# A RetNet recurrence feeding a SiLU feed-forward layer: how the remainders of split operands are formed, four buffers for g, and the reload of chunk 2's x

## The chip, the cores and the metric

The kernel runs on one core of one Trainium2 chip. The metric is the device time in microseconds of one execution; lower is better. TensorE (PE) multiplies, and loads its weights on a second track (PEld). VectorE (DVE), ScalarE (ACT) and GpSimd (POOL) work element by element, and SyncE (SP) issues all DMAs, in one queue.

## The reference

```
# q, k, v: (4, 8, 768, 64); gamma[h] = 1 - 2**(-5-h); scale = 1/8
for t in range(768):
    state = gamma * state + outer(k[:, :, t], v[:, :, t])
    y[:, :, t] = scale * q[:, :, t] @ state
x = y.transpose(0, 2, 1, 3).reshape(3072, 512)
h = x @ w_in            # 512 x 2048
g = h * sigmoid(h)
out = g @ w_out         # 2048 x 512
```

The inputs are given to the kernel as 64-bit words; it builds 32-bit floats from them where they are weights.

## The kernel before, in words

The sequence is cut into six chunks `c` of 128 steps, and four batches `b` give 24 units `n = 4c + b`. A unit's attention has three stages, visited one behind another: `visit(m)` runs the transposes of unit m (`stage_t`, for early units on PE), the scores and state sums of unit m-1 (`stage_s`, `stage_a`), and the outputs of unit m-2 (`stage_y`). From unit 14 (`FAR`) on the transposes are made by DMA instead: `part_t` (POOL copies), `turn_t` (two DMA transposes, to tiles kw and qw), `join_t` (ACT copies).

A chunk's four y make x^T of that chunk. Every operand of the two large products is kept in three parts (high, low, and a scaled combination), so that three products of rounded numbers give the accuracy of one of full ones. So a product (c, f), with f one of the 16 slices of w_in, has 12 matmuls of 512 columns: 8 into bank `ha`, 4 into `hb` (`multiply`, L749). `close_steps` (L775) takes them out: ACT copies `ha` to an SBUF tile `g` (L777), DVE subtracts `hb` (L782), and `put_g` stores `g` to DRAM. `turn` hands out three PSUM banks in rotation, `h0` to `h2`; four others hold attention's tiles, tagged s and y, and one, q, is used by the early transposes and at the very end.

The order of the products is written out in `steps`: chunks 0 and 1 with the early slices, chunk 2 with slices 0 to 7 among them, then `last`: (0, 12) to (0, 15), (1, 12) to (1, 15), (2, 8) to (2, 15), then chunks 3, 4 and 5. `behind[c, f]` gives the work that is issued behind a product; `visit(14)` stands behind (1, 15). PE's order is the program's; the orders of the other engines come from a scheduler, within the queues that `queue(...)` and `tc.issue_after` set. `behind_next` holds work for DVE behind the next drain.

`takes` names the products behind which one slice of weights is converted from 64-bit words (`convert_steps`, L199 to L231: two ACT and four DVE operations, the last a custom one on 16-bit words at L230). Slices of w_in are then split into parts (`split_steps`, L115): ACT makes the high part (L121), DVE a remainder into a tile `wl` (L124), ACT the low part by scaling the remainder (L127), DVE the third (L129). Slices of w_out go to DRAM and are read back and split the same way during chunk 5. The factor 1/8 of the reference is put into w_in's parts.

Chunk 2's x has no room to stay: its place is needed for the last four slices of w_in. Its four quarters go to DRAM (`y_dram`), and come back when chunk 0's x is done: `late_y(b)` reloads quarter b into a tile `yr`, `late_x(b)` splits it again (ACT high part L653, DVE L656 and L659). (2, 8) is the first product that reads the reloaded x, and every one of its matmuls reads columns of all four quarters. The tiles `kt` (two buffers) and `qt` (three) are shared among transposed k and q, the copies for the DMA transposes, and these reloads. A buffer is free when the last reader of its tile has run.

When all `g` are stored they are read back, put through SiLU and split (L843 to L847), and multiplied with w_out (L1270).

Of the kernel before, what the change touches and what calls it, by code (L numbers as in the profile page):

```python
# [12 lines left out]

FP32 = mybir.dt.float32
FP32R = mybir.dt.float32r
# [3 lines left out]
AF = mybir.ActivationFunctionType  # L19
ALU = mybir.AluOpType  # L20
# [8 lines left out]
EPS = 2.0 ** -12  # L29
# [5 lines left out]
def kernel(  # L35
# [46 lines left out]
    def pool(name, bufs, **kw):  # L82
        return ctx.enter_context(tc.tile_pool(name=name, bufs=bufs, **kw))
# [4 lines left out]
    const = pool("const", 1)  # L88
    ld = pool("ld", 2)
    one = pool("one", 1)  # L90
    hpool = pool("hpool", 3)
    stage = pool("stage", 2)
    conv = pool("conv", 1)
    ps_u = pool("ps_u", 1, space=PS)
# [17 lines left out]
            quads[name] = wpool.tile([128, 4, 3, 512], FP32R, tag="wq", name=f"{name}4")  # L112
        return quads[name][:, f - NF + 4]

    def split_steps(f, w32, name, factor, to, behind_x=False):  # L115

        to[f] = w = w_slot(f, name)
        lo = conv.tile([128, 512], FP32, tag="wl", name=f"{name}l_{f}")
        yield
        with queue((held or evac or [None])[0] if behind_x or f >= NF - 4 else evac[0]):  # L120
            nc.scalar.activation(out=w[:, 0, :], in_=w32, func=AF.Copy, scale=HALF * factor)  # L121
        high = w[:, 0, :].bitcast(FP32)
        yield
        nc.vector.scalar_tensor_tensor(out=lo, in0=w32, scalar=factor, in1=high,  # L124
                                       op0=ALU.mult, op1=ALU.subtract)
        yield
        nc.scalar.activation(out=w[:, 1, :], in_=lo, func=AF.Copy, scale=1.0 / EPS)  # L127
        yield
        nc.vector.scalar_tensor_tensor(out=w[:, 2, :], in0=high, scalar=EPS, in1=lo,  # L129
                                       op0=ALU.mult, op1=ALU.subtract)  # L130

    def split_w(*of):
        steps = split_steps(*of)
        next(steps)
        yield
        list(steps)
# [17 lines left out]
    def load(name, n):  # L154
        if n >= len(units):
            return
        c, b = units[n]
        src = {"k": k, "q": q, "v": v}[name]
        if n == 4 * B and name == "k":
            t = conv.tile([128, H, D], FP32, tag="wl", name=f"kf_{n}")  # L160
            nc.sync.dma_start(out=t, in_=src[b, :, ds(c * C, C)].rearrange("h t d -> t h d"))
            kqv[name][n] = t
            return
        if n < EARLY:

            if n not in early:
                early[n] = wpool.tile([128, 3, H, D], FP32, tag=f"w{4 + n}", name=f"kqv_{n}")
            t = early[n][:, "kqv".index(name)]
        else:
            t = ld.tile([128, H, D], FP32, tag=f"{name}f", name=f"{name}f_{n}",  # L170
                        bufs=2 if name == "q" else 3)
        nc.sync.dma_start(out=t, in_=src[b, :, ds(c * C, C)].rearrange("h t d -> t h d"))
        kqv[name][n] = t
# [76 lines left out]
    def early_slice(i):  # L250

        out = []
        yield from convert_steps(i, out)
        yield
        steps = split_steps(i, out[0], "wi", scale, w_sb, None)
        next(steps)
        yield from steps

# [9 lines left out]
    def take_w(after=None, parts=False):  # L268

        i = taken[0]  # L270
        taken[0] += 1
        if i >= 2 * NF:
            return
        with queue(after) if after else ExitStack():
            rounded = convert_w(i)

        def finish():
            w32 = rounded()
            if i < NF:
                list(split_w(i, w32, "wi", scale, w_sb))  # L280
            else:
                to_store.append((i - NF, w32))

        if parts:
            behind_next.append(finish)
        else:
            with queue(after) if after else ExitStack():
                finish()
# [13 lines left out]
    def begin_w():  # L302

        i = taken[0]
        taken[0] += 1
        split = split_w(i, convert_w(i)(), "wi", scale, w_sb, True)
        next(split)
        half_split.append(split)

# [93 lines left out]
    def turn(name):  # L403
        turns[0] += 1
        return ps_h.tile([128, 512], FP32, tag=f"h{turns[0] % 3}", name=name)
# [271 lines left out]
    y_late = {}  # L677

    def late_y(b):
        p, tag, bufs = ((one, "kt", 2), (conv, "wl", 1))[b % 2]  # L680
        y_late[b] = p.tile([128, KIN, C], FP32, tag=tag, name=f"yr_{b}", bufs=bufs)
        nc.sync.dma_start(out=y_late[b], in_=y_dram[b])

# [62 lines left out]
    def product_in(c, f):  # L746
        close_in(c, f, *multiply(c, f))

    def multiply(c, f):  # L749
        ha, hb = turn(f"ha_{c}_{f}"), turn(f"hb_{c}_{f}")  # L750
        fill(ha, FILL_P.get((c, f), 0))
        for i in range(3):
            for kk in range(KIN):
                nc.tensor.matmul(hb if i == 2 else ha, lhsT=w_sb[f][:, i, ts(kk, 128)],  # L754
                                 rhs=woven(xt[c][:, i, kk, :]), start=kk == 0 and i != 1,
                                 stop=kk == KIN - 1 and i != 0)
        return ha, hb
# [16 lines left out]

    def close_steps(c, f, ha, hb):  # L775
        hs = new_g(c, f)
        copied[:] = [nc.scalar.activation(out=hs, in_=ha, func=AF.Copy, scale=ONE_E).ins]  # L777
        with queue(copied[0]):
            while behind_copy:
                behind_copy.pop(0)()  # L780
        yield
        taken_out[:] = [nc.vector.tensor_tensor(out=hs, in0=hs, in1=hb, op=ALU.subtract).ins]  # L782
        with queue(taken_out[0]):
            while behind_next:
                behind_next.pop(0)()
        yield
        (later if (c, f) in kept_g else pending).append((c, f, hs))
# [31 lines left out]
            w_got[f] = t  # L819

    def w_out(f, parts=False):
        steps = split_steps(f, w_got.pop(f), "wo", 1.0, wo)
        for _ in range(3):
            next(steps)
        get_w(f + W_READ)
        if parts:
            behind_next.append(lambda: list(steps))
        else:
            list(steps)
# [323 lines left out]
    takes = [(1, 5)] + [(0, f) for f in range(6, half)]  # L1153
    takes += [(2, half - 4), (2, half - 2)]
    takes += [(0, half), (0, half + 3), (1, half + 1), (1, half + 3)]
    takes += [(0, NF - 3), (0, NF - 1), (1, NF - 3)]
    takes += [(3, f) for f in (0, 3, 7, 11, 14)]
    takes += [(4, f) for f in (0, 3, 7, 11, 14)]
    takes += [(5, f) for f in (2, 5, 8)]
# [6 lines left out]
    for i, x in enumerate(at):  # L1166
        behind[x] = lambda m=EARLY + 6 + i: visit(m)
    behind[0, NF - 2] = lambda: [late_y(b) for b in range(2)]
    behind[1, NF - 4] = lambda: [late_x(0), late_y(2), late_x(1), late_y(3)]
    behind[1, NF - 2] = lambda: [late_x(2), late_x(3)]  # L1170
    behind[1, NF - 1] = lambda: visit(EARLY + 6)


# [11 lines left out]
    put_later = {6: 1, 7: 2, 9: 1, 10: 1, 11: 1, 13: 1, 14: 1, 15: 1}  # L1185
    assert sum(put_later.values()) == len(kept_g)
    loads_at = {first_far + 4: [("k", FAR + 1), ("q", FAR + 1)], far[FAR] + 1: [("q", FAR + 2)]}
    for n, (c, f) in enumerate(steps):
        if n in scales_at:
            behind_next.append(lambda m=scales_at[n]: scale_k(m))  # L1190
        if n in joins_at:
            behind_copy.insert(0, lambda m=joins_at[n]: [join_t(name, m) for name in "qk"])
        if n in parts:
            behind_next.append(lambda m=parts[n]: part_t(m, taken_out[0]))
        patient[0] = steps.index((3, 0)) <= n < max(turns_at) + 2
        product_in(c, f)
        put_g(1)
        if n in put_later:
            put_g(len(later) - put_later[n], later)
        store_w()  # L1200
        if (c, f) in takes:
            take_w(taken_out[0], n < len(pairs + three) or c == NC - 1)
        behind.get((c, f), lambda: None)()
        if n in turns_at:
            turn_t(turns_at[n])
            if turns_at[n] >= LATER:
                with tc.issue_after(turned_by[0]):
                    load("k", turns_at[n] + 1), load("q", turns_at[n] + 1)
        if turns_at.get(n - 1, 0) >= LATER:
            with tc.issue_after(stored[0]):  # L1210
                load("v", turns_at[n - 1] + 1)
        if turns_at.get(n - 2, 0) >= LATER:
            with tc.issue_after(stored[0]):
                while waiting:
                    load_w(waiting.pop(0))
        for name, m in loads_at.get(n, ()):
            load(name, m)
        if c == NC - 1:
            if f == 0:
                for i in range(W_READ):  # L1220
                    get_w(i)
            if f < NF - 4:
                w_out(f, True)
            if f >= NF - 6:
                if f == NF - 6:
                    for n in range(G_AHEAD):
                        get(n)
                if f >= NF - S_AHEAD:
                    with tc.issue_after(taken_out[0]):
                        split(f - NF + S_AHEAD)  # L1230
# [124 lines left out]
```

## Time and profile before

| | |
|---|---|
| runs | 593.3, 593.84 and 3425.35 us; median 593.84 |
| the profiled execution | 592.68 us, its span 590.9 |
| PE, DVE, ACT, POOL busy | 579.3, 401.1, 342.7, 34.1 us |
| DMA | 108.91 MB, mean 184 GB/s |

The profile is of one execution. Times within it are microseconds from the start of the span. An engine's idle time matters only where another waits for it; PE's matters always where PE sets the end.

### The profile page before, as it was taken

How to read it: one execution, taken by the hardware profiler on the slowest of the kernel's cores; microseconds unless marked ns; L12 is line 12 of the kernel's file. 1: busy time of each engine (PE TensorE's matmuls, PEld its weight loads, DVE VectorE, ACT ScalarE, POOL GpSimd, SP SyncE). 2: the span in 40 equal slices, each digit the busy share in tenths (PEclk: the TensorE clock that was granted, in tenths of full speed). 3: DMA queues.
4: the chain of work that ended last, by engine and by line, in shares of the span. 5: the costliest groups of instructions: out<-in, count | busy, mean ns of one | idle time of the engine just before them, and what ended most of it. 6: DMA issues, size and time to landing. Idle time of an engine off the chain costs nothing. (4 is left out here: it accounts for less than half of the span.)

```text
span 590.9 us, 13700 instructions
## 1 busy us (share of the span) xinstructions
PE 579.3 (98%) x5509; PEld 498.2 (84%) x5509; DVE 401.1 (68%) x672; ACT 342.7 (58%) x607; POOL 34.1 (6%) x89
## 2 busy tenths in 40 slices
PE   8999999999999999999999999999999999999996
PEld 6787888888788888888888888888888888888885
DVE  3887999678896767767779794745645463645632
ACT  7787767576656446655477695544644544545311
POOL 3000120100022111120000000000000000000000
PEclk9999999999999999999999999999999999999999
DMA  9989877786699699999667863532524433443301
GB/s 193 214 198 207 191 194 266 251 251 215 202 263 222 174 269 245 285 258 253 236 207 276 265 214 107 175 111 91 194 73 138 147 108 106 158 127 102 113 1 72
DMA packets 144336, 108.91 MB, mean 184 GB/s; under 512 B 101136, under 2 KB 109584, under 8 KB 144272
## 3 DMA queue, kind: packets, MB, share of 16 engines
q1 hardware_dynamic: 144272, 108.03, 65.3%
q8 instruction: 43, 0.70, 0.5%
q14 instruction: 21, 0.17, 0.1%
HBM read 66.06 MB, written 36.70 MB: 174 GB/s over the span
## 5 line engine op out<-in xcount | busy, mean ns | idle before, releaser
L754 PE MATMUL ha<-xt,wi 128*128 128x512 f32 x736 | 176.6, 382 | 0.6 <-DVE g L782 0.4
L754 PEld LDWEIGHTS ha<-xt,wi 128*128 128x128 f32 x736 | 137.1, 189 | 22.6 <-DVE g L782 2.6
L1270 PE MATMUL o<-wo,gs 128*128 128x512 f32 x564 | 137.1, 379 | 0.0
L1270 PEld LDWEIGHTS o<-wo,gs 128*128 128x128 f32 x564 | 106.6, 189 | 15.1
L846 DVE TENSOR_TENSOR gs<-gr,gs 128x512 fp32r<-128x512 f32 x96 | 62.1, 685 | 83.1 <-ACT gs L844 83.1
L1270 PE MATMUL oa<-wo,gs 128*128 128x512 f32 x376 | 111.8, 379 | 0.0
L843 ACT ACTIVATE gr<-gr 128x512 f32<-128x512 f32 x96 | 59.6, 629 | 65.5 <-DMA gr<-gd 64.2
L754 PE MATMUL hb<-xt,wi 128*128 128x512 f32 x368 | 95.0, 380 | 1.8 <-DVE gk L782 0.9
L777 ACT ACTIVATE g<-ha 128x512 f32<-128x512 f32 x87 | 51.8, 596 | 64.1 <-PE ha L754 49.8
L782 DVE TENSOR_TENSOR g<-g,hb 128x512 f32<-128x512 f32 x87 | 59.5, 684 | 41.7 <-ACT g L777 34.6
L754 PEld LDWEIGHTS hb<-xt,wi 128*128 128x128 f32 x368 | 69.1, 189 | 13.5 <-DVE gk L782 1.7
L1270 PEld LDWEIGHTS oa<-wo,gs 128*128 128x128 f32 x376 | 71.1, 189 | 10.1
L844 ACT ACTIVATE gs<-gr 128x512 fp32r<-128x512 f32 x96 | 53.3, 621 | 38.2 <-PE ob L1270 29.9
L1270 PE MATMUL ob<-wo,gs 128*128 128x512 f32 x188 | 71.3, 379 | 0.0
L847 DVE SCALAR_TENSOR_TENSOR gs<-gs 128x512 fp32r<-128x512 f32 x96 | 61.9, 683 | 0.1
L1270 PEld LDWEIGHTS ob<-wo,gs 128*128 128x128 f32 x188 | 35.5, 189 | 5.0
L211 ACT ACTIVATE ca<-wf 128x512 f32<-128x512 f32 x32 | 26.5, 827 | 20.1 <-DVE cs L224 11.2
L542 DVE TENSOR_TENSOR am<-sc,decay 128x512 f32<-128x512 f32 x24 | 16.5, 686 | 10.2 <-PE sc L534 8.7
L224 DVE SCALAR_TENSOR_TENSOR cs<-ca,cs 128x512 uint32<-128x512 uint32 x32 | 22.1, 690 | 0.8
L659 DVE SCALAR_TENSOR_TENSOR xt<-xt 128x512 fp32r<-128x512 f32 x28 | 20.8, 755 | 0.6
L582 PE MATMUL y<-qt,mid 64*64 64x64 f32 x376 | 19.4, 220 | 1.0 <-issue 1.0
L1319 DVE TENSOR_TENSOR o<-o,o 128x512 f32<-128x512 f32 x10 | 6.7, 687 | 17.4 <-ACT o L1318 17.4
(136 smaller groups left out, 611.3 us busy)
## 6 DMA issues: line engine op xcount, KB each, us to landing
gr<-gd SPq DMA_DIRECT2D x96, 256.0 KB, 2.8
gd<-g SPq DMA_DIRECT2D x87, 256.0 KB, 3.9
wf<-in_moe_w_out_dram SPq DMA_DIRECT2D x16, 512.0 KB, 4.6
out_dram<-o SPq DMA_DIRECT2D x23, 256.0 KB, 2.5
wf<-in_moe_w_in_dram SPq DMA_DIRECT2D x16, 256.0 KB, 4.2
wf<-in_moe_w_in_dram SPq DMA_DIRECT2D x32, 128.0 KB, 4.1
kf<-in_k_dram SPq DMA_DIRECT2D x16, 256.0 KB, 4.9
qf<-in_q_dram SPq DMA_DIRECT2D x16, 256.0 KB, 4.5
```

The source lines that it names most:

```text
L211: top = nc.scalar.activation(out=a.bitcast(FP32), in_=hi.bitcast(FP32), func=AF.Abs, scale=2.0 ** -3).ins
L224: nc.vector.scalar_tensor_tensor(out=s, in0=a, scalar=3, in1=s, op0=ALU.logical_shift_left, op1=ALU.bitwise_xor)
L582: i = nc.tensor.matmul(to[ts(e, D), o, a, :], lhsT=lhsT, rhs=rhs, start=key not in started, stop=True, skip_group_check=True).ins
L659: nc.vector.scalar_tensor_tensor(out=x[2], in0=x[1].bitcast(FP32), scalar=-1.0 / EPS, in1=x[0].bitcast(FP32), op0=ALU.mult, op1=ALU.add)
L754: nc.tensor.matmul(hb if i == 2 else ha, lhsT=w_sb[f][:, i, ts(kk, 128)], rhs=woven(xt[c][:, i, kk, :]), start=kk == 0 and i != 1, stop=kk ...
L777: copied[:] = [nc.scalar.activation(out=hs, in_=ha, func=AF.Copy, scale=ONE_E).ins]
L782: taken_out[:] = [nc.vector.tensor_tensor(out=hs, in0=hs, in1=hb, op=ALU.subtract).ins]
L843: nc.scalar.activation(out=g, in_=g, func=AF.Silu)
L844: nc.scalar.activation(out=t[:, 0, :], in_=g, func=AF.Copy, scale=HALF)
L846: nc.vector.tensor_tensor(out=t[:, 1, :], in0=g, in1=high, op=ALU.subtract)
L847: nc.vector.scalar_tensor_tensor(out=t[:, 2, :], in0=t[:, 1, :].bitcast(FP32), scalar=-1.0 / EPS, in1=high, op0=ALU.mult, op1=ALU.add)
L1270: nc.tensor.matmul(o, lhsT=g, rhs=woven(wo[f][:, i, :], (c, b) == (NC - 1, B - 1)), start=f == 0 and i != 1, stop=f == NF - 1 and i != 0 o ...
```

## The change

- The remainders of a slice are formed by DVE alone. A custom operation computes (a - b) times a factor; it makes the low part from the input and the high part, and the third from high and low. The tile `wl` and ACT's copy at L127 go. The factor 1/8 leaves w_in's parts: `close_steps` applies it when it takes out `ha` (in ACT's scale) and `hb` (a scalar-tensor-tensor on DVE in place of a tensor-tensor).
- `g` has four buffers (`hs`) instead of three. One early k tile and one reload use them too.
- From the eighth entry of `steps` on every second product puts `hb` in bank q, so that products alternate between two pairs of banks.
- The third and fourth quarters of chunk 2's reload are issued behind (0, 15) instead of (1, 12), the fourth into a `qt` buffer, the second into an `hs` buffer; the splits stand behind (1, 12) and (1, 13) instead of (1, 12) and (1, 14).
- Three slices of w_out are converted behind (2, 10), (2, 12) and (2, 15) instead of (0, 13), (0, 15) and (1, 13).

```diff
-    hpool = pool("hpool", 3)
+    hpool = pool("hpool", 4)
...
-    def split_steps(f, w32, name, factor, to, behind_x=False):
+    def difference(out, a, b, factor):
+        nc.vector._custom_dve(TENSOR_TENSOR_REDUCE_SUB_MAX, out=out, in0=a, in1=b, s1=factor)
+
+    def split_steps(f, w32, name, to, behind_x=False):
         to[f] = w = w_slot(f, name)
-        lo = conv.tile([128, 512], FP32, tag="wl", name=f"{name}l_{f}")
+        high, low = (w[:, i, :].bitcast(FP32) for i in range(2))
         yield
         with queue((held or evac or [None])[0] if behind_x or f >= NF - 4 else evac[0]):
-            nc.scalar.activation(out=w[:, 0, :], in_=w32, func=AF.Copy, scale=HALF * factor)
-        high = w[:, 0, :].bitcast(FP32)
-        yield
-        nc.vector.scalar_tensor_tensor(out=lo, in0=w32, scalar=factor, in1=high,
-                                       op0=ALU.mult, op1=ALU.subtract)
-        yield
-        nc.scalar.activation(out=w[:, 1, :], in_=lo, func=AF.Copy, scale=1.0 / EPS)
-        yield
-        nc.vector.scalar_tensor_tensor(out=w[:, 2, :], in0=high, scalar=EPS, in1=lo,
-                                       op0=ALU.mult, op1=ALU.subtract)
+            nc.scalar.activation(out=w[:, 0, :], in_=w32, func=AF.Copy, scale=HALF)
+        yield
+        difference(w[:, 1, :], w32, high, 1.0 / EPS)
+        yield
+        difference(w[:, 2, :], high, low, EPS)
...
-            t = conv.tile([128, H, D], FP32, tag="wl", name=f"kf_{n}")
+            t = hpool.tile([128, H, D], FP32, tag="hs", name=f"kf_{n}")
...
-        p, tag, bufs = ((one, "kt", 2), (conv, "wl", 1))[b % 2]
+        p, tag, bufs = ((one, "kt", 2), (hpool, "hs", 4), (one, "kt", 2), (one, "qt", 3))[b]
...
+    by_q = []
...
-        ha, hb = turn(f"ha_{c}_{f}"), turn(f"hb_{c}_{f}")
+        ha = turn(f"ha_{c}_{f}")
+        hb = banks("q", f"hb_{c}_{f}", 1)[:, 0] if (c, f) in by_q else turn(f"hb_{c}_{f}")
...
-        copied[:] = [nc.scalar.activation(out=hs, in_=ha, func=AF.Copy, scale=ONE_E).ins]
+        copied[:] = [nc.scalar.activation(out=hs, in_=ha, func=AF.Copy,
+                                         scale=scale * ONE_E).ins]
...
-        taken_out[:] = [nc.vector.tensor_tensor(out=hs, in0=hs, in1=hb, op=ALU.subtract).ins]
+        taken_out[:] = [nc.vector.scalar_tensor_tensor(
+            out=hs, in0=hb, scalar=-scale, in1=hs, op0=ALU.mult, op1=ALU.add).ins]
...
-    takes += [(0, NF - 3), (0, NF - 1), (1, NF - 3)]
+    takes += [(2, NF - 6), (2, NF - 4), (2, NF - 1)]
...
     behind[0, NF - 2] = lambda: [late_y(b) for b in range(2)]
-    behind[1, NF - 4] = lambda: [late_x(0), late_y(2), late_x(1), late_y(3)]
-    behind[1, NF - 2] = lambda: [late_x(2), late_x(3)]
+    behind[0, NF - 1] = lambda: [late_y(b) for b in range(2, B)]
+    behind[1, NF - 4] = lambda: [late_x(b) for b in range(2)]
+    behind[1, NF - 3] = lambda: [late_x(b) for b in range(2, B)]
...
+    by_q += steps[len(pairs) + 1 :: 2]
```

More of the change, by code (lines that the diff above doesn't have):

```diff
@@ L12 @@
 from concourse._compat import with_exitstack
+from concourse.dve_ops import TENSOR_TENSOR_REDUCE_SUB_MAX
 FP32 = mybir.dt.float32
@@ L254, in early_slice @@
         yield
-        steps = split_steps(i, out[0], "wi", scale, w_sb, None)
+        steps = split_steps(i, out[0], "wi", w_sb, None)
         next(steps)
@@ L279, in finish @@
             if i < NF:
-                list(split_w(i, w32, "wi", scale, w_sb))
+                list(split_w(i, w32, "wi", w_sb))
             else:
@@ L305, in begin_w @@
         taken[0] += 1
-        split = split_w(i, convert_w(i)(), "wi", scale, w_sb, True)
+        split = split_w(i, convert_w(i)(), "wi", w_sb, True)
         next(split)
@@ L821, in w_out @@
     def w_out(f, parts=False):
-        steps = split_steps(f, w_got.pop(f), "wo", 1.0, wo)
+        steps = split_steps(f, w_got.pop(f), "wo", wo)
         for _ in range(3):
```

## The prediction

> **What bounds the kernel now.** I read the page's busy shares first, then the stretches, then the order of time around each break in the matmuls.
>
> ```profile
> span 590.9 us, 13700 instructions
> PE 579.3 (98%) x5509; PEld 498.2 (84%) x5509; DVE 401.1 (68%) x672; ACT 342.7 (58%) x607; POOL 34.1 (6%) x89
> 337.58 1.29 PE o L1270 x6
> ```
>
> PE is busy all along and sets the end: whatever the change is worth must show as PE time won or lost. Matmuls overlap, so that a busy PE can still lose time; I take the issue interval from the chain that ended last: six matmuls in 1.29 us, 0.215 us each. Four take 0.86 us and eight 1.73 us; a group that starts later than that after the one in front has lost the difference.
>
> The stretches show where the other engines have room:
>
> ```profile
> 60.00:100.00 40.00, 39.04 (x633) 32.03 (x622) 38.33 (x64) 26.56 (x50) 5.56 (x9) 1.00 0.79 217
> 100.00:150.00 50.00, 50.00 (x233) 43.66 (x232) 39.54 (x66) 32.59 (x51) 2.02 (x2) 1.00 0.77 238
> 180.00:200.00 20.00, 20.00 (x330) 17.38 (x329) 12.35 (x22) 11.15 (x18) 2.51 (x4) 1.00 1.07 220
> 290.00:355.00 65.00, 64.73 (x300) 56.35 (x300) 55.87 (x92) 48.75 (x86) 0.00 (x0) 1.00 0.74 241
> ```
>
> After the length come PE, PEld, DVE, ACT and POOL. DVE has 1.7 us left of 40 at 60 to 100 us, 10.5 of 50 behind it, 9.1 of 65 at 290 to 355. ACT has room everywhere. The breaks among the products, in order of time:
>
> ```profile
> 157.80 0.83 DVE L230 CUSTOM_DVE_ANT_0 cw<-wf,cs 128x1024 uint16<-128x1024 uint16 x1 [1.48 <-DMA wod<-cw]
> 157.88 1.03 PE L754 MATMUL hb<-xt,wi 128*128 128x512 f32 x4
> 159.29 1.99 PE L754 MATMUL ha<-xt,wi 128*128 128x512 f32 x8 [0.38 <-DVE g L782]
> 161.12 1.03 PE L754 MATMUL hb<-xt,wi 128*128 128x512 f32 x4
> 162.28 1.99 PE L754 MATMUL ha<-xt,wi 128*128 128x512 f32 x8
> 164.03 0.63 ACT L653 ACTIVATE xt<-yr 128x512 fp32r<-128x512 f32 x1 [2.11 <-DMA yr<-yd]
> 165.07 0.69 PE L582 MATMUL y<-am,vf 64*64 64x64 f32 x32
> 167.09 1.99 PE L754 MATMUL ha<-xt,wi 128*128 128x512 f32 x8
> 169.64 1.10 PE L754 MATMUL hb<-xt,wi 128*128 128x512 f32 x4 [0.55 <-DVE xt L659]
> 331.69 1.89 PE L754 MATMUL ha<-xt,wi 128*128 128x512 f32 x8
> 333.86 1.13 PE L754 MATMUL hb<-xt,wi 128*128 128x512 f32 x4 [0.27 <-ACT g L777]
> ```
>
> Lost: 159.29 - 157.88 - 0.86 = 0.55; 162.28 - 161.12 - 0.86 = 0.30; 169.64 - 167.09 - 1.73 = 0.82; 333.86 - 331.69 - 1.73 = 0.44. A group behind a wait also lasts 0.10 longer (1.99 against 1.89), or 0.07 at 169.64 (1.10 against 1.03).
>
> **The change part by part.**
>
> *Two pairs of banks, four `hs` buffers, w_out slices later: minus 1.6 us.* The first break is a queue of causes: DVE's sum of a w_out slice waits 1.48 us for a store, the drain of the product in front stands behind it, and that drain frees PE's bank. With pairs a bank is free one whole product (12 x 0.215 = 2.6 us) after its drain is due, and the three slices are gone from here. The break at 333.86 is ACT waiting for a `g` buffer whose store had not landed; a fourth buffer gives it one product more. I take the breaks at 159, 162 and 333 with their restarts: 0.65 + 0.40 + 0.54 = 1.6. Bounds: nothing, and all that weight loads of products waited for these two drains:
>
> ```profile
> PEld ha L754 <- DVE g L782: 2.6, 6, 0.8
> PEld hb L754 <- ACT g L777: 1.3, 3, 0.7
> ```
>
> which is 3.9. The three slices return among chunk 3's visits, each with four DVE operations (at the 0.83 of the longest, quoted at 157.80, 3.3 us at most) and two of ACT:
>
> ```profile
> L211 ACT ACTIVATE ca<-wf 128x512 f32<-128x512 f32 x32 | 26.5, 827 | 20.1 <-DVE cs L224 11.2 <-DMA wf<-in_moe_w_out_dram 6.4 <-DMA wf<-in_moe_w_in_dram 2.5
> ```
>
> about 1.7 us. The stretch 180 to 200 has 7.6 and 8.8 free per 20 us, so nothing is added; uncovered it is at most today's 0.65 + 0.40 again, and today's break is the likelier shape: none.
>
> *Scaled remainders on DVE: nothing.* 32 ACT copies go, but ACT is not what PE waits for. DVE keeps two operations per slice, now the custom subtract-and-scale twice, and `close_steps` has a scalar-tensor-tensor for a tensor-tensor.
>
> ```profile
> L124 DVE SCALAR_TENSOR_TENSOR wil<-cs,wi x16: 682/691/1485, 16.6 to 148.4; 128x512 f32<-128x512 f32 x16
> L230 DVE CUSTOM_DVE_ANT_0 cs<-cs,cw x16: 673/689/1541, 12.0 to 146.1; 128x1024 uint16<-128x1024 uint16 x16
> L847 DVE SCALAR_TENSOR_TENSOR gs<-gs 128x512 fp32r<-128x512 f32 x96 | 61.9, 683 | 0.1
> ```
>
> No row has this custom operation. The nearest is the other custom one: median 689 ns, shortest 673, longest 1541. I take 0.69, as for the operation it replaces, because both medians and the two-input row at L847 agree on that. Its upper bound matters for a rival below.
>
> *Chunk 2's x: minus 0.8, then plus 7.0 us.* Today's break in the first product of (2, 8) goes (0.82 with its restart, since the third part no longer ends last). The new one is in the buffers. `late_y(3)` takes a `qt` buffer. There are three, and at that time they hold qt_12, qt_13 and kw_14 (chunk 14's turned k, kept until `join_t` behind (2, 8)). qt_12 is read last by the closing products of `stage_y(12)`, and those stand in `visit(14)`, which PE runs between (1, 15) and (2, 8). So the reload of the fourth quarter can't be issued before that visit has ended on PE, and (2, 8), the next thing on PE, needs that quarter in its first matmul. In the built order of SP the reload stands, moreover, behind the store of g(1, 15), the load of v and the DMA transpose of unit 15's q, which waits for POOL's copies. Now it is issued well before the visit and ACT's high part of it ends by then.
>
> The length, from the visit's start on PE (V = 165.07 in this trace):
>
> ```profile
> 166.15 0.09 POOL L412 MEMSET token<- 1x1 f32 x1 [51.18 <-PE y L582]
> 112.96 1.04 POOL L444 COPY qp<-qf 128x1024 uint16<-128x1024 uint16 x1 [27.77 <-issue]
> 167.45 1.50 POOL L444 COPY qp<-qf 128x1024 uint16<-128x1024 uint16 x1
> 171.45 1.36 SPq L455 DMA_TRANSPOSE qw<-qp  x1
> 182.98 2.01 SPq L455 DMA_TRANSPOSE kw<-kp  x1
> 172.90 0.53 SPq L172 DMA_DIRECT2D qf<-in_q_dram  x1
> 176.62 1.12 POOL L444 COPY qp<-qf 128x1024 uint16<-128x1024 uint16 x1 [2.15 <-DMA qf<-in_q_dram]
> DMA to landing us min/median/max: 2.6/3.9/4.4
> ```
>
> POOL's token ends at V + 1.17. Two copies at 1.04 (112.96, DVE not in the way) bring V + 3.2; as they ended in this visit, at 167.45 + 1.50 = 168.95, it is V + 3.9. The transpose's issue with its gap is 1.45 (171.45 to 172.90): V + 4.65, where the reload is issued. A load of the same size issued behind a transpose (172.90) let its reader start at 176.62, 3.7 later: V + 8.35. The last row is the reload's own landing time now. ACT's high part adds 0.63: PE goes on at V + 9.0. The visit ends at 167.09, V + 2.02. PE idles 7.0 us. The lower parts follow within the eight matmuls of `ha` (1.73 us against two DVE operations of 0.69), so nothing is late behind it. Bounds: shortest copies, a transpose issue of 1.3 and a landing of 2.6 give 5.8; slow copies, a transpose issue of 2.0 (182.98) and a landing of 4.4 give 9.0.
>
> *The clock behind the stall: plus 2.0 us.*
>
> ```profile
> 0.99 1.22 PE L329 MATMUL idle<-zero 128*128 128x32 bf16 x39 [0.99 <-DVE zero L317]
> 4.30 0.90 PE L492 MATMUL kp<-ident,kqv 128*128 128x128 f32 x4 [0.19 <-POOL step L374]
> 82.03 0.60 PE L492 MATMUL kp<-ident,kf 128*128 128x128 f32 x4
> 585.80 0.46 PE oa L1294 x4
> 589.00:591.00 2.00, 0.00 (x0) 0.00 (x0) 0.00 (x0) 0.00 (x0) 0.00 (x0) 0.50 0.05 16
> ```
>
> The last matmuls end at 586.26, and from 589 on the granted clock (the third number from the end of the row) is 0.50: an idle of 2.7 us was enough. At the start the four transposes at 4.30 still take 0.90 instead of 0.60 although PE has worked since 0.99, so a cold PE stays slow for about 4 us. A stall of 7.0 us is longer than the one; the other costs half of its 4 us: 2.0. Bounds: nothing if the clock holds; 3.0 (an estimate: half as much again) as the phase of the restart is unknown.
>
> [...]
>
> *Sum.* The profiled execution took 592.68 (span 590.9, 1.8 around it). 592.68 - 1.6 - 0.8 + 7.0 + 2.0 = 599.3. Two runs of before, 593.3 and the median 593.84 (the third, 3425.35, stands alone), lie 0.6 and 1.2 above the profiled one, so as a median I say **600.0**. Bounds: 592.68 - 3.9 - 0.8 + 5.8 = 593.8 and 592.68 - 0.8 + 9.0 + 3.0 + 1.05 = 604.9.
>
> **The rivals.**
>
> *The clock holds.* 599.3 - 2.0 = 597.3, as a median 598.0. For it: the clock is 1.00 in every stretch above. Against: no stretch has an idle PE this long, and the tail shows the fall.
>
> *The reload gets out in time.* Then only the gains are left: 592.68 - 1.6 - 0.8 = 590.3, a median of 591.0; this is also what the change says of itself. It needs qt_12 to be free before the visit, or so short a reload that the visit's 2.0 us hide it; the shortest landing is 2.6 and ACT's 0.63 comes on top. Three quarters of x do come sooner, which helps nothing while (2, 8) needs all four.
>
> *The custom operation is slow, and DVE becomes the bound.* Place: where the slices are split, counted by line 124, which opens each remainder:
>
> ```profile
> 60.00:100.00 40.00, 4.23 (x5) 1.00 0.79 217
> 100.00:150.00 50.00, 5.54 (x8) 1.00 0.77 238
> 290.00:355.00 65.00, 11.04 (x16) 1.00 0.74 241
> ```
>
> Two operations each: 10, 16 and 32. At 1.1 us each (0.41 over) the first stretch overflows by 4.1 - 1.7 = 2.4 and the last by 13.1 - 9.1 = 4.0: 599.3 + 6.4 = 605.7, and from there it is over 2% slower; at the longest row, 1.54, it is 6.8 + 3.1 + 18.1 = 28 more (the middle term is 13.6 - 10.5 at 100 to 150 us). Against it: the medians at L124, L230 and L847.
> [...]
>
> **How the numbers follow.** Stall with a cold clock 0.68 (600.0); stall with the clock held 0.16 (598.0); reload in time 0.10 (591.0); DVE the bound, or a stall that spreads, 0.06 (over 605.7). The likeliest gives the time. 593.8 to 604.9 are the bounds of the sum; they leave out the third case and the fourth: 593.5 to 605. Two per cent is 11.9 us, about what a measurement of this kernel can tell from no change. Faster by that needs 582, beyond even all gains: 0.01. Slower takes the fourth case: 0.06. Within: 0.93.
>
> **What would show it.** Right: one break of 6 to 9 us between the last `y` matmul of the visit and the first `ha` of (2, 8), released by ACT `xt`<-`yr`, which waited for the DMA; a granted clock below 1 right behind it; no break at (1, 14), (1, 15) and near 333; L118 at about 690 ns. Wrong: (2, 8) starting within 1 us of the visit, or DVE above 95% at 290 to 355.

## The result, and the profile after

The changed kernel takes 601.84 us (median of 598.24, 600.52, 603.15 and 603.19) against 593.87 before: a ratio of 1.0143, 95% interval 1.0115 to 1.0172. It is slower, by less than two per cent. The profiled execution took 603.15 us, 10.47 more than that of before. In the changed kernel the lines have moved: the product's matmuls are L758 (were L754), the drains L781 and L787 (L777, L782), the conversion copy L212 (L211), the high part of x L654 (L653).

The page of the changed kernel, its head, and below it the view of PE's waits (total, times, longest):

```profile
span 601.4 us, 13661 instructions
PE 579.8 (96%) x5509; PEld 500.1 (83%) x5509; DVE 400.9 (67%) x672; ACT 324.8 (54%) x575; POOL 33.6 (6%) x89
```

```profile
PE ha L758 <- ACT xt L654: 7.5, 1, 7.5
PE ha L758 <- ACT g L781: 3.7, 3, 1.9
```

PE is busy as long as before (579.3); the span is 10.5 longer, and nearly all of it is PE standing still, in four places. ACT has lost the 32 copies (342.7 to 324.8), and nothing shows for it in PE's time. The timeline of the changed kernel around the first place; the last number of a row is the idle time before it and what ended it:

```profile
163.39 0.69 PE L583 MATMUL y<-am,vf 64*64 64x64 f32 x32
164.47 0.09 POOL L413 MEMSET token<- 1x1 f32 x1 [49.88 <-PE y L583]
164.75 1.04 POOL L445 COPY kp<-kf 128x1024 uint16<-128x1024 uint16 x1 [0.19 <-DMA gd<-g]
165.26 0.22 PE L583 MATMUL y<-qt,state 64*64 64x64 f32 x2
165.73 1.04 POOL L445 COPY qp<-qf 128x1024 uint16<-128x1024 uint16 x1
166.80 2.58 SPq L456 DMA_TRANSPOSE qw<-qp  x1
169.43 0.57 SPq L683 DMA_DIRECT2D yr<-yd  x1
172.27 0.63 ACT L654 ACTIVATE xt<-yr 128x512 fp32r<-128x512 f32 x1 [6.11 <-DMA yr<-yd]
172.96 3.67 PE L758 MATMUL ha<-xt,wi 128*128 128x512 f32 x8 [7.47 <-ACT xt L654]
```

Read from the top: the visit, POOL's two copies, the DMA transpose on SP, the reload of the fourth quarter behind it, its landing, ACT's high part, and only then (2, 8). The visit ends on PE at 165.48, and the reload leaves at 169.43: 4.0 us of the way lie between the end of the visit and the reload's turn in SP's queue, 2.8 behind its issue. The eight matmuls of `ha` then take 3.67 us instead of 1.89. The stretches of the changed kernel say why (the granted clock is the third number from the end):

```profile
169.00:170.00 1.00, 0.00 (x0) 0.00 (x0) 0.00 (x0) 0.00 (x0) 0.00 (x0) 0.78 0.08 17
170.00:176.00 6.00, 3.04 (x7) 2.51 (x8) 1.38 (x2) 0.63 (x1) 0.00 (x0) 0.50 0.25 66
176.00:177.00 1.00, 1.00 (x5) 0.83 (x5) 0.00 (x0) 0.34 (x1) 0.00 (x0) 0.81 0.00 0
180.00:200.00 20.00, 20.00 (x448) 17.57 (x448) 18.68 (x32) 13.64 (x21) 4.78 (x7) 1.00 1.11 236
```

The rows at 168 to 169 and 177 to 180 read 1.00, the one at 170 to 176 0.50. Between these two, a mean of 0.78 over one us is half clock for 0.44 of it, so the clock was half from 169.56 to 176.38. PE worked in that from 172.96 on: 3.42 us at half speed, 1.71 lost.

The three other places were not foreseen. PE, then ACT, in the timeline of the changed kernel:

```profile
213.84 1.03 PE L758 MATMUL hb<-xt,wi 128*128 128x512 f32 x4
215.95 1.99 PE L758 MATMUL ha<-xt,wi 128*128 128x512 f32 x8 [1.09 <-ACT g L781]
227.78 1.03 PE L758 MATMUL hb<-xt,wi 128*128 128x512 f32 x4
229.60 1.99 PE L758 MATMUL ha<-xt,wi 128*128 128x512 f32 x8 [0.80 <-ACT g L781]
266.56 1.03 PE L758 MATMUL hb<-xt,wi 128*128 128x512 f32 x4
269.45 1.99 PE L758 MATMUL ha<-xt,wi 128*128 128x512 f32 x8 [1.86 <-ACT g L781]
```

```profile
213.27 0.88 ACT L212 ACTIVATE ca<-wf 128x512 f32<-128x512 f32 x1 [3.83 <-DMA wf<-in_moe_w_out_dram]
226.89 0.88 ACT L212 ACTIVATE ca<-wf 128x512 f32<-128x512 f32 x1 [5.40 <-DMA wf<-in_moe_w_out_dram]
267.16 0.73 ACT L212 ACTIVATE ca<-wf 128x512 f32<-128x512 f32 x1 [6.13 <-DMA wf<-in_moe_w_out_dram]
```

ACT reaches the first copy of a w_out slice before the slice has landed, and the drain of `ha` that PE needs stands behind that copy on the same engine. By the prediction's way of counting (start to start, less 0.86 for four matmuls) PE loses 1.25, 0.96 and 2.03: 4.2 us. Counted through the copies from (2, 10) on, these are not the three moved slices but later ones, those taken behind (3, 0), (3, 3) and (4, 0). The first of them follows the moved slice of (2, 15) by a single product; in before it waited for no transfer. The copies behind (3, 3) and (4, 0) waited in before too (3.33 us at 216.76 and 3.10 at 254.97), without a break over 0.25 us on PE.

What went, in PE's timeline of the changed kernel, and the custom operation in the view of the tile `wi` (min/median/max ns):

```profile
159.84 1.03 PE L758 MATMUL hb<-xt,wi 128*128 128x512 f32 x4
160.70 1.89 PE L758 MATMUL ha<-xt,wi 128*128 128x512 f32 x8
162.43 1.03 PE L758 MATMUL hb<-xt,wi 128*128 128x512 f32 x4
...
332.25 1.89 PE L758 MATMUL ha<-xt,wi 128*128 128x512 f32 x8
333.97 1.03 PE L758 MATMUL hb<-xt,wi 128*128 128x512 f32 x4
```

```profile
L118 DVE CUSTOM_DVE_ANT_0 wi<-cs,wi x16: 680/691/1477, 16.7 to 147.3; 128x512 fp32r<-128x512 f32 x16
L118 DVE CUSTOM_DVE_ANT_0 wi<-wi x16: 680/691/695, 17.9 to 148.0; 128x512 fp32r<-128x512 f32 x16
```

The groups follow one another at 0.86 and 1.73: the breaks near 159, 162 and 333 are gone. The bill of the two profiled executions: 7.5 for the stall, 1.7 for the clock, 4.2 for slices that landed late, less 1.6 and 0.8 for breaks that went, is 11.0 against 10.47 measured. The difference lies ahead of the visit: it starts at 163.39 instead of 165.07, 1.7 earlier, of which the breaks at 159 and 162 account for 1.05; the other 0.6 was won ahead of them.

### The profile page after: what moved, and what is told of

It is laid out like the page before. It is cut to its first block, busy times and chain, and to the rows that moved or that the text cites. A ratio compares the mean times of both kernels' runs of the same rounds, so it can differ in the third digit from the quotient of the medians.

```text
span 601.4 us, 13661 instructions
## 1 busy us (share of the span) xinstructions
PE 579.8 (96%) x5509; PEld 500.1 (83%) x5509; DVE 400.9 (67%) x672; ACT 324.8 (54%) x575; POOL 33.6 (6%) x89
## 4 chain that ended last, share of the span: by engine, by line
PE 76%; DVE 7%; DMA 7%; ACT 4%; issue 3%; SPq 2%; POOL 0%; DVEq 0%; ACTq 0%
PE ha L758 20%; PE o L1278 20%; PE oa L1278 13%; PE hb L758 10%; PE ob L1278 7%; DMA wf<-in_moe_w_out_dram 3%; PE y L583 2%; SPq L173 1%; DVE xt L657 1%; DMA wod<-cw 1%; DMA yr<-yd 1%; PE sc L525 1%; PE sc L535 1%; DMA kqv<-in_q_dram 1%; DVE cs L215 1%
## 5 line engine op out<-in xcount | busy, mean ns | idle before, releaser
L758 PE MATMUL ha<-xt,wi 128*128 128x512 f32 x736 | 178.0, 385 | 11.5 <-ACT xt L654 7.5
L758 PEld LDWEIGHTS ha<-xt,wi 128*128 128x128 f32 x736 | 138.4, 190 | 33.4 <-ACT xt L654 7.6
L758 PE MATMUL hb<-xt,wi 128*128 128x512 f32 x368 | 94.6, 380 | 0.9 <-DVE gk L787 0.9
L781 ACT ACTIVATE g<-ha 128x512 f32<-128x512 f32 x87 | 51.6, 597 | 75.6 <-PE ha L758 73.1
L787 DVE SCALAR_TENSOR_TENSOR g<-hb,g 128x512 f32<-128x512 f32 x87 | 59.8, 688 | 42.4 <-ACT g L781 27.0
L758 PEld LDWEIGHTS hb<-xt,wi 128*128 128x128 f32 x368 | 69.5, 189 | 11.5 <-DVE gk L787 1.7
L212 ACT ACTIVATE ca<-wf 128x512 f32<-128x512 f32 x32 | 26.1, 816 | 29.1 <-DMA wf<-in_moe_w_out_dram 17.7
L660 DVE SCALAR_TENSOR_TENSOR xt<-xt 128x512 fp32r<-128x512 f32 x28 | 19.0, 687 | 0.5
L215 DVE TENSOR_SCALAR cs<-wf 128x512 uint32<-128x512 uint32 x32 | 18.3, 572 | 0.0
```

The costliest lines, as they stand in the source:

```text
L212: top = nc.scalar.activation(out=a.bitcast(FP32), in_=hi.bitcast(FP32), func=AF.Abs, scale=2.0 ** -3).ins
L215: nc.vector.tensor_scalar(out=s, in0=hi, scalar1=0x80000000, scalar2=None, op0=ALU.bitwise_and)
L787: taken_out[:] = [nc.vector.scalar_tensor_tensor(out=hs, in0=hb, scalar=-scale, in1=hs, op0=ALU.mult, op1=ALU.add).ins]
```

## The experiments

The theory: the changed kernel loses its time to the reload that waits for a `qt` buffer, and the rest to the three slices moved late, which make transfers collide. The rivals: the slices alone, the bank pairs, the custom operation.

**The fourth quarter into another buffer.** Only the buffer of `late_y(3)` differs; `cw` is free at that time.

```diff
-        p, tag, bufs = (..., (one, "qt", 3))[b]
+        p, tag, bufs = (..., (conv, "cw", 1))[b]
```

> The changed kernel with one edit: the fourth quarter of chunk 2's reload goes into the idle buffer cw of the slice conversion instead of a qt buffer. Theory (the stall before (2, 8) is the wait for qt_12's buffer, 7.5 us, and the half clock behind it, about 1.8): both go, 601.8 - 9.3 = 592.5 us, and the granted clock stays 1.00 to the last matmul. Rival (the quarter is late for another reason, the queue of DMAs or ACT): a break of over 3 us stays in front of (2, 8) and the time stays above 597. The breaks between 215 and 270 us in the trace after (3.7 us) should stay in both.

Measured: 594.29 us, ratio to before 1.0021 (1.001 to 1.0033), where the changed kernel has 1.0143. The reload in SP's queue, and PE's timeline of this kernel around the visit and at the breaks that are left:

```profile
158.16 0.32 SPq L683 DMA_DIRECT2D yr<-yd  x1
...
165.50 0.65 PE L535 MATMUL sc<-qt,kt 64*64 64x64 f32 x32
166.31 1.99 PE L758 MATMUL ha<-xt,wi 128*128 128x512 f32 x8
...
207.84 1.99 PE L758 MATMUL ha<-xt,wi 128*128 128x512 f32 x8 [1.30 <-ACT g L781]
...
260.26 1.99 PE L758 MATMUL ha<-xt,wi 128*128 128x512 f32 x8 [1.85 <-ACT g L781]
```

The last reload now leaves at 158.16, ahead of the visit, and (2, 8) follows the visit at once. The profiled executions differ by 603.15 - 593.99 = 9.2 us, as much as the 7.5 of the stall and the 1.7 of the clock together. That they agree so well is partly luck: this execution had lost 0.9 more by 68 us, and lacks the 0.96 of (3, 3). The buffer is the cause of the stall and of the cold clock. Two of the three later breaks stay, those at (3, 0) and (4, 0); all three were expected to.

**The three slices back in their old places**, all else as changed.

```diff
-    takes += [(2, NF - 6), (2, NF - 4), (2, NF - 1)]
+    takes += [(0, NF - 3), (0, NF - 1), (1, NF - 3)]
```

> The changed kernel with the three w_out slices back behind (0, 13), (0, 15) and (1, 13). Theory (the breaks of 1.1, 0.8 and 1.9 us between 215 and 270 us come from conversions pressed into the stretch of the DMA transposes, where ACT waits for a slice's words in front of the drains): these breaks go, minus 4 us. The reload of the fourth quarter here stands ahead of the transpose of unit 15's q in the built order of SP, still behind the visit's last products; so its stall should be about 7.5 less 2.7 = 4.8 us with the clock still dropping: 601.8 - 4 - 2.7 = 595 us (596.9 if the clock is cold for longer, 593.3 if it holds). Rival (the breaks are the doing of the stall or of the bank pairs): they stay, 599.

Measured: 602.19 us, ratio 1.0147 (1.0126 to 1.0168): no gain, a miss. SP's queue and PE in the timeline of this kernel:

```profile
168.44 2.40 SPq L802 DMA_DIRECT2D gd<-g  x1
...
172.14 1.73 SPq L683 DMA_DIRECT2D yr<-yd  x1
...
177.45 3.78 PE L758 MATMUL ha<-xt,wi 128*128 128x512 f32 x8 [9.49 <-ACT xt L654]
```

The breaks by ACT's `g` went, as expected, but the same stall grew from 7.5 to 9.5 us where 4.8 was expected. This time no transpose stands ahead of the reload; a w_out slice's load and store, a store of `g` (168.44) and two loads do, and the reload is issued at 172.14. What the reload stands behind in SP's queue has changed; that it stands there has not. The stall's growth alone doesn't eat up the 4.2 us of the breaks: this execution, the slowest of four, was also 2.4 us behind the changed kernel's profile by 70 us, through an early break of 1.45 us with half clock behind it (see the end), nearly 100 us ahead of the first of the three slices. So the profile doesn't say what the return of the slices is worth here; the median shows no gain.

**Both at once**: the slices back and the fourth quarter in an `hs` buffer.

```diff
-        p, tag, bufs = (..., (one, "qt", 3))[b]
+        p, tag, bufs = (..., (hpool, "hs", 4))[b]
-    takes += [(2, NF - 6), (2, NF - 4), (2, NF - 1)]
+    takes += [(0, NF - 3), (0, NF - 1), (1, NF - 3)]
```

> The changed kernel with the slices back as in the run before this one and the fourth quarter in an hs buffer like the second. Theory (reload and late slices are all that costs): no break over 0.5 us behind 100 us, the gains alone remain, 590 to 591.5 us, some 0.4 to 0.6% under the kernel before. Rival (the custom operation or the drains cost too): 593.9 or more.

Measured: 592.38 us, ratio 0.9987 (0.9963 to 1.001): all of the loss is gone, though the 590 to 591.5 that was expected isn't reached; and 1.9 us less than with `cw` and late slices, in the same comparison. What the slices and what the other buffer bring of the 1.9 isn't separated. In its trace, which is that of its slowest execution (595.52), the break at (3, 0) is gone, as in the experiment before, but two breaks over 0.5 us are there, in the first product of (2, 8) and at (4, 0), where none was expected:

```profile
169.64 1.13 PE L758 MATMUL hb<-xt,wi 128*128 128x512 f32 x4 [1.27 <-DVE g L787]
261.86 2.00 PE L758 MATMUL ha<-xt,wi 128*128 128x512 f32 x8 [2.72 <-ACT g L781]
```

So the break at (3, 0) appears only with the moved slices: the changed kernel and the one with `cw` have it, the two without them don't (and one more trace with them, of the kernel with zeros below, doesn't have it either). The one at (4, 0) comes without them too: ACT's copy at 259.64 waited 7.12 us for its slice. Why that slice landed late stays open.

**The kernel before, with the slices late.**

```diff
-    takes += [(0, NF - 3), (0, NF - 1), (1, NF - 3)]
+    takes += [(2, NF - 6), (2, NF - 4), (2, NF - 1)]
```

> The kernel before with one edit: three w_out slices behind (2, 10), (2, 12), (2, 15) instead of (0, 13), (0, 15), (1, 13). Theory (late slices cost by themselves): breaks of over 0.7 us between 200 and 270 us in front of products, released by ACT drains that stood behind a wait for wf; plus 4, minus the breaks at 159 and 162 us (1.05): 593.9 + 3 = 597 us. Rival (they only cost behind a stall that has pushed the DMAs together): 593 us, under the kernel before by the two breaks.

Measured: 597.17 us, ratio 1.0083 (1.0048 to 1.0118). The profile is that of the fastest of its seven executions (594.82); a further execution of the same kernel shows a slower one.

> The kernel of e4_before_late once more, for the profile of a typical execution (its first profile was the fastest of seven, 594.82, against a median of 597.17). Theory: ACT's conversion copy of a late slice waits for wf's landing in front of the drains, so that PE breaks by 2 to 5 us behind (2, 10), (2, 12) or (2, 15), with a granted clock below 1 there where a break passes about 4 us; time 596 to 600. Rival: the breaks stay under 1 us and the time is lost elsewhere.

Measured: 599.32 us. The timeline and the stretches of this execution:

```profile
49.44 0.27 PE L582 MATMUL y<-qt,mid 64*64 64x64 f32 x1 [2.27 <-issue]
...
204.53 0.60 ACT L777 ACTIVATE g<-ha 128x512 f32<-128x512 f32 x1 [5.20 <-DMA gd<-g]
205.18 1.13 PE L754 MATMUL hb<-xt,wi 128*128 128x512 f32 x4 [3.84 <-ACT g L777]
```

```profile
206.50:207.00 0.50, 0.50 (x38) 0.50 (x30) 0.47 (x2) 0.50 (x2) 0.00 (x0) 0.60 1.10 270
...
210.00:211.00 1.00, 1.00 (x6) 0.86 (x6) 1.00 (x2) 1.00 (x2) 0.00 (x0) 0.99 2.52 212
```

At the place of the slices there is one break of 3.84 us, and a clock at half for 3.4 us behind it. The "about 4 us" from which a break should cost clock was the author's estimate; it is not shown as a bound, as the clock fell behind 2.27 us too (below). The mechanism was not the expected one. With three `hs` buffers ACT doesn't wait for the slice but for the store of an earlier `g`, whose buffer it needs; the other execution has the same break, 3.09 us at 201.94. The moved slices put their loads and stores into a stretch where the DMA share was 1.07 before (180 to 200). That this is what makes the store late is a reading, not shown by a run. With three buffers it is a store of `g` that comes late, with four the next slice.

That the time of this execution lies in the expected 596 to 600 is partly luck. Of the 6.6 us that it took more than the profiled one of before, 3.6 were lost ahead of 72 us: the first row is a break in attention, far ahead of the slices, which has 1.03 us in before (47.44) and 2.27 here, with a half clock of 3.4 us behind it. The other execution of this very kernel is 2.5 us earlier at that point. What the slices cost is therefore read from the rest. In both traces the breaks near 159 and 162 are gone and also the one in the first product of (2, 8), though the reload is the old one, about 2.1 us by 172 us; behind that, 3.6 us (594.82) and 5.3 us (599.32) are lost by 280 us.

**PE kept busy through the stall**: 26 products with zeros ahead of (2, 8), all else as changed.

```diff
-    FILL_P = {(0, 0): 1, (1, 0): 2}
+    FILL_P = {(0, 0): 1, (1, 0): 2, (2, 8): 26}
```

> The changed kernel with 26 multiplications of a zero tile put on PE ahead of the first matmul of (2, 8), into the bank that this product is about to overwrite. They take 26 x 0.215 = 5.6 us of the 7.5 us stall and change nothing else. Theory (the stall is followed by a cold clock that costs half of its 3.6 us of work): the granted clock stays 1.00 there and the time falls by 1.8 us, to 600.0 if after is 601.8; the break that is left is about 2 us. Rival (the cold clock costs nothing, as later work waits for other things anyway): no difference, 601.8.

Measured: 601.97 us, ratio 1.0147 (1.013 to 1.0164), no gain in the median. PE's timeline of this kernel and its stretches:

```profile
165.47 5.79 PE L324 MATMUL ha<-zero 128*128 128x512 bf16 x26
172.91 1.99 PE L758 MATMUL ha<-xt,wi 128*128 128x512 f32 x8 [1.66 <-ACT xt L654]
...
199.56 0.65 PE L758 MATMUL ha<-xt,wi 128*128 128x512 f32 x1 [2.67 <-issue]
```

```profile
171.00:176.00 5.00, 3.35 (x16) 2.74 (x15) 1.52 (x3) 1.69 (x3) 0.00 (x0) 1.00 0.12 45
199.00:200.00 1.00, 0.44 (x1) 0.36 (x2) 0.00 (x0) 0.00 (x0) 0.00 (x0) 0.87 1.26 250
...
203.00:204.00 1.00, 1.00 (x6) 0.89 (x5) 0.96 (x2) 0.00 (x0) 0.00 (x0) 0.92 1.44 239
```

On the spot it did what the theory says: the clock stayed at 1.00, PE resumed at the same time (172.91 and 172.96), and the eight matmuls took 1.99 instead of 3.67, 1.7 us less. Of the three breaks by late slices this execution has none, though it takes the slices in the same late places; so these breaks come and go. In their stead it has one of 2.67 us at 199.56, inside a product, for which the profile names no releaser, with half clock behind it. The clock's price is shown at its place; in the median of the whole time it is not.

**The bank pairs alone**, on the kernel before.

```diff
-        ha, hb = turn(f"ha_{c}_{f}"), turn(f"hb_{c}_{f}")
+        ha = turn(f"ha_{c}_{f}")
+        hb = banks("q", f"hb_{c}_{f}", 1)[:, 0] if (c, f) in by_q else turn(f"hb_{c}_{f}")
...
+    by_q += steps[len(pairs) + 1 :: 2]
```

> The kernel before with the bank pairs alone. Theory of the prediction (the breaks at 159 and 162 us are drains late for a bank, and so is the one at 333 for its second half): these go, minus 1 to 1.6 us, a ratio of 0.9973 to 0.9983. Rival (the drains catch up anyway, or the breaks move): 1.000.

Measured: 595.09 us, 591.32 to 600.16, ratio 1.005 (1.0029 to 1.007): slower, a miss. The profiled execution is the fastest of the ten; the breaks near 159, 162 and 333 are gone in it. A further execution:

> The kernel of e6_pairs once more, for the profile of a typical execution (its first profile was the fastest of ten, 591.32, against a median of 595.09). Theory: the pairs make products run ahead, so that a later wait is longer: breaks of 2 us or more at one or two places around (1, 14) to (2, 9) or in 290 to 355, with a time of 594 to 597. Rival: no breaks beyond those of the first profile, the difference spread over the span as longer matmul intervals.

Measured: 591.76 us, in PE's timeline:

```profile
169.52 1.13 PE L757 MATMUL hb<-xt,wi 128*128 128x512 f32 x4 [0.91 <-DVE xt L659]
```

This is the old break of (2, 8), longer than the 0.55 of before; no other break between 150 and 355 us is over 0.3. So both traces show a gain as expected (591.32 and 591.76), while the other nine executions took 594.13 to 600.16, and none of those has a trace. Where they lose it stays open.

**The remainders alone**, on the kernel before: the custom operation in `split_steps`, and the factor 1/8 moved to `close_steps`, as in the change.

```diff
-        nc.vector.scalar_tensor_tensor(out=lo, in0=w32, scalar=factor, in1=high, ...)
...
+        difference(w[:, 1, :], w32, high, 1.0 / EPS)
...
+        difference(w[:, 2, :], high, low, EPS)
```

> The kernel before with the remainders on DVE alone and the factor moved to the drains, and nothing else (the tile wl stays for its loads). Theory (off the path: custom operation 0.68 to 0.69 us as the one it replaces, ACT's 20 us not waited for): ratio 0.999 to 1.001. Rival 1 (ACT's relief brings drains forward): 0.995 to 0.998. Rival 2 (DVE in front of PE at 60 to 150 us): 1.002 or more.

Measured: 592.87 us, ratio 0.9999 (0.9984 to 1.0013). They cost nothing and bring nothing that can be told from zero, within 0.2%. The profiled execution of this kernel was one of its slowest (595.25): it lost 1.1 us more than before by 69 us and 2.2 us more between 180 and 226 us.

**Pairs and remainders together**, with three `hs` buffers, the old reloads and the old places of the slices (the diffs of the last two).

> The kernel before with both the bank pairs and the remainders, three g buffers, the old reload and the old places of the slices: what is left of the change when its two costly parts are taken out. Theory (gains of the pairs, remainders free): 0.997 to 0.9985, and faster than both the kernel before and the changed one. Rival (gains do not add up or are used up elsewhere): 1.000.

Measured: 594.88 us, 590.11 to 598.18, ratio 1.0026 (1.0006 to 1.0046): as the pairs alone, with a like spread, and a miss: it was expected to be faster than before. Its profiled execution (593.94) is the fifth of twelve and so nearer to the median than the two of the pairs alone. In it the breaks near 159, 162 and 333 are gone, and 2.5 us are lost against before between the visits at 180 and 226 us (180.70 to 225.85 before, 180.14 to 227.75 here), in breaks of 0.64 (188.25), 0.34 (189.99), 0.23 (199.12) and 0.41 us (222.37). But the slow execution of the remainders alone loses 2.2 in the same stretch without pairs, so this isn't shown to be the price of the pairs. In the kernel with four `hs` buffers and the pairs ("both at once") the spread is 590.68 to 595.52. A fourth buffer may be what the pairs need; no run separates that.

**Both at once, without the pairs.**

```diff
-    by_q += steps[len(pairs) + 1 :: 2]
```

> The changed kernel with the fourth quarter reloaded into an hs buffer and the three slices of w_out back behind (0, 13), (0, 15) and (1, 13), as in e3_both, and without the bank pairs (hb in the three rotating banks everywhere). If the pairs cost what e6_pairs and e8_keep suggest (0.3 to 0.5%, 2 us), this gives 590 to 591.5, ratio 0.993 to 0.997, and beats both kernels. Rival: in e3_both the four hs buffers already take that cost away; then it is the same as e3_both or the breaks at 159 to 162 come back: 592.4 to 593.5, ratio 0.999 to 1.001.

Measured: 591.79 us, ratio 0.9984 (0.9963 to 1.0005); the interval still holds 1. More executions of the same kernel:

> The kernel of e9_no_pairs once more, with more runs, as its interval (0.9963 to 1.0005) still held 1. If the four hs buffers and the remainders on DVE are worth what its trace shows (breaks of 1.0 us in all between 150 and 348 us, against 1.4 before, and none at 333), it is 591 to 592.5 against 593 to 593.9, ratio 0.997 to 0.999 with an interval that ends below 1. Rival: the difference was chance, ratio 0.999 to 1.001.

Measured: 591.53 us against 592.65, ratio 0.9974 (0.9959 to 0.9989). Its breaks in PE's timeline between 150 and 355 us:

```profile
158.51 1.13 PE L758 MATMUL hb<-xt,wi 128*128 128x512 f32 x4 [0.69 <-ACT g L781]
167.67 1.97 PE L758 MATMUL ha<-xt,wi 128*128 128x512 f32 x8 [0.55 <-DVE g L787]
```

The break near 333 is gone, and the wait in the first product of (2, 8) now stands ahead of its first matmul (0.55) instead of its third part. What of the change brings the quarter of a per cent isn't shown. The fourth buffer need not be it: the break near 333 is missing too in the traces of the pairs alone and of the remainders alone, which have three. This is the one version here whose interval lies below the kernel before, in the second series; in the first it still held 1. It isn't shown to beat the one with the pairs (0.9987).

## Why the prediction was right, and where its sum was not

- *The chain of the stall: right.* From the visit's start at 163.39 the token ended at V + 1.17 as said, the copies at 3.4 (3.2), the reload was issued at 6.0 (4.65), its reader started at 8.9 (8.35), PE at 9.6 (9.0). Two errors nearly cancelled: the DMA transpose with its gap held SP for 2.63 us, not 1.45, and outside even the bound of 2.0; the reload's reader started 2.84 behind its issue, not 3.7. So a part of the agreement is luck. PE idled 7.47 where 7.0 stood, in 5.8 to 9.0. The first experiment shows that the buffer makes the stall: with another one the reload leaves 11 us earlier.
- *The clock: right, a little too dear.* 1.71 where 2.0 stood: PE worked at half speed for 3.42 us (172.96 to 176.38), where about 4 had been estimated from the start of before. The 3.0 of the upper bound was the author's estimate, and no run shows it. The rival in which the clock holds is refuted by the stretches from 169 to 177 (0.50 at 170 to 176).
- *Remainders on DVE: right.* 691 ns at L118 for both forms, the replaced operation's own median; alone, the ratio is 0.9999. DVE is busy for 400.9 us in all (401.1 before), and for 52.56 of 65 us at 290 to 355, where over 95% was to speak for the rival of the slow operation. That rival falls with this; the 1.1 us per operation that it was worked out with was the author's estimate.
- *Late slices at nothing: wrong, and the failing step of the sum.* The prediction bounded them by today's two breaks, 1.05. Put alone into the kernel before, they cost 4.1 us in the median (597.17 against 593.03), net of the breaks that they remove; in the changed kernel's profile the break at (3, 0), 1.25, goes with them, and between the two kernels with another buffer the median moved by 1.9, of which the other buffer may have a share. The other 3.0 of that profile, the slices of (3, 3) and (4, 0), had no term in the sum at all. The argument counted free DVE and ACT time in 180 to 200. That cover exists in part (ACT 13.64 and DVE 18.68 of 20 in the changed kernel, where the work stands some 7 us later), but it isn't what counts: ACT stood idle *because* a slice or a store had not landed, with a drain queued behind. The row that might have warned was the DMA share of 1.07 in the very stretch that was quoted for its free time.
- *Breaks won, minus 1.6 and minus 0.8: right in the trace, not confirmed in the median.* All four breaks are gone. The reasons are only in part those of the prediction. The pairs alone remove those near 159 and 162, but the moved slices alone do so too. The 0.8 in (2, 8) was put down to the earlier reload; it goes with the moved slices under the old reload, and with the earlier reload and the old slices a wait there remains (1.27 and 0.55 in two kernels). The one near 333, put down to the fourth `g` buffer, is missing in other traces with three. The pairs alone are slower by half a per cent in the median, and without pairs the version above keeps 1.1 us of the gain.
- *The total.* 599.3 stood for the profiled execution and 603.15 came: 4.2 for the slices and 0.5 for the stall are missing, 0.3 is too much for the clock, and the 0.6 won ahead of the visit had no term either. In the median 600.0 stood and 601.84 came, inside 593.5 to 605; two of the other three executions were faster than the profiled one (598.24 and 600.52). They have no traces; that some of the breaks were missing in them would fit.

## What to carry to other kernels

Before a buffer is given to a load, find the last reader of the tile in it and where that reader stands in its engine's order: if that is right ahead of the load's own consumer, the engine waits for the whole way from one to the other, however early the load is written in the program (7.5 us here). When work is moved to a stretch with idle engines, read the DMA share of that stretch (1.07 here) and what each engine's next instruction waits for: ACT's drains stood behind copies that waited 3.8 to 6.1 us for a slice, and idle time of that kind is no room. And before a time is put down to one edit, compare the two traces at a point ahead of it: here executions of one kernel were up to 2.5 us apart by 72 us.

## What the runs showed of the hardware

In the traces that show a half clock it came in steps. The mixed rows give its length: 3.42 us in the filled kernel (199.74 to 203.16), 3.42 in the second execution with the late slices (206.60 to 210.02), 6.82 in the changed kernel (169.56 to 176.38), and 10.24 with the slices put back (171.50 to 181.74), from these rows of that kernel's stretches (the first row belongs to its early break):

```profile
48.00:49.00 1.00, 0.71 (x8) 0.65 (x9) 0.30 (x1) 0.32 (x1) 0.00 (x0) 0.81 0.30 53
...
171.00:172.00 1.00, 0.00 (x0) 0.00 (x0) 0.00 (x0) 0.00 (x0) 0.00 (x0) 0.75 0.92 322
...
181.00:182.00 1.00, 1.00 (x4) 0.86 (x3) 0.00 (x0) 0.73 (x2) 0.00 (x0) 0.63 0.00 0
```

These lengths are one, one, two and three times about 3.41 (6.82 / 2, 10.24 / 3). The early breaks have one of 3.4 us each: from 48.62 with the slices put back, behind 1.45 us of idle PE, and from 49.60 in the second execution with the late slices, behind 2.27. In three cases the half clock began only when PE worked again: 0.2 us behind the restart at 199.56, 0.3 behind that at 48.29, and 1.4 us behind that at 205.18. So breaks of 1.45, 2.27, 2.67 and 3.84 us had 3.4 us of half clock behind them, which costs up to 1.7 us more (an estimate: half of 3.42, where PE works all through it). In the fastest execution with late slices a break of 3.09 us cost no clock (mean 1.000 over the span). What decides between the two isn't shown.

The idle time of a break was therefore, in these runs, the lower end of its price (7.47 us idle and 1.71 of clock in the changed kernel). And SP was held for 2.58 us by a DMA transpose (166.80), where the two rows quoted of before have 1.36 and 2.01.
